# Strassen's scheme for the second layer's second product, in two of its three pairs of token blocks

## The chip, the cores and the metric

The kernel runs on one core of one Trainium2 chip. The metric is the device time of one execution in microseconds, as the median of several executions.

## The reference

Three stages follow each other. An attention with keys and values pooled by 8 (4 x 8 heads, 576 positions, 64 wide) gives x with 2304 rows and 512 columns. A gated layer follows. The last stage is a mixture of 8 experts whose weights per token come from eight rounds of normalisation:

```python
x = _moe_ref(x)                      # (sigmoid(x @ w_gate) * (x @ w_val)) @ w_out, 512 -> 1536 -> 512
N, D = x.shape                       # 2304, 512
P = exp(logits - max); 8 rounds of row and column normalisation      # logits = x @ w_gate, (N, 8)
out = np.zeros((N, D))
for e in range(E):                   # E = 8
    h = np.maximum(x @ w1[e], 0.0)   # 512 -> 1024: the first product
    ye = h @ w2[e]                   # 1024 -> 512: the second product
    out += P[:, e:e + 1] * ye
```

All is float32. The kernel reaches that accuracy on TensorE by splitting each operand into a high and a low half (type float32r) and by adding three products of halves: high x high, high x low and low x high (`PASSES`, L252).

## The kernel before, in words

**Tiling.** The 2304 tokens are six blocks of 384 (`TB`), taken in three pairs. The last stage ("second layer") runs in 96 steps, `steps2` (L657): for each pair of blocks p, each expert e and each quarter q of the expert's hidden columns one step n. The hidden quarter is 2 x 128 columns. Pair 0 is steps 0 to 31, pair 1 steps 32 to 63, pair 2 steps 64 to 95.

**First product.** In a step, x @ w1 for two blocks of tokens, two halves of the inner width and two halves of the hidden quarter is a 2 x 2 by 2 x 2 product of blocks. It is made by the Strassen-Winograd scheme with seven products instead of eight: P1, P5, P6, P3, P7, P2, P4, in this order, called by `product` (L887). Each is 2 (inner) x 3 (passes) = 6 matmuls with 128 x 128 weights and 384 moving columns. The sums of x for it, `xf` (seven tiles a pair, loaded at the end of the pair before by `load_xf`, L714, as soon as the product that reads the old tile is done), come from a scratch memory in DRAM. The sums of w1 are made in each step for the next step by `prep_w1` (L675): ScalarE makes the high halves, GpSimd the sums and the low halves, into the tiles `fa` and `fs`. The raw w1 is loaded two steps ahead by `load_w1` (L661).

**Evacuation.** The results of the products meet in PSUM: `c1`, `c5` and `c2` are copied to SBUF by ScalarE (L1003, L1011, L1018) and added back by VectorE (L1024, L1030, L1037). `hidden` (L905) makes the two halves of the Relu of each block, the high one on ScalarE (L909), the low one on VectorE (L910).

**Second product.** `y_chunk` (L914) makes for one tile of 128 tokens the whole h @ w2 of one hidden quarter: 2 (hidden halves) x 3 (passes) = 6 matmuls, the h tile as weights and 512 columns of w2 moving, into one PSUM bank ("big", four of them). VectorE then adds it, times P, to the accumulator `acc` (L955, first time L941). A step has six such chunks, those of the step before, one behind each of six of the seven products. w2 is split by `prep_w2` (L703): ScalarE makes the high half (L708), VectorE the low one (L709). It is loaded one step ahead by `load_w2` (L667). After the last step the last six chunks run by themselves.

**Order.** The order of the instructions on every engine is the order of this program text (a manual schedule). All DMAs are issued by SP, in order; an issue that waits for a buffer or for a result holds back those behind it. In the first twelve steps the normalisation of P (`sinkhorn`, L833) runs between the chunks.

Of the kernel before, what the change touches and what calls it, by code (L numbers as in the profile page):

```python
# [20 lines left out]
def attention_moe_moe_kernel(  # L21
# [31 lines left out]
    nc = tc.nc  # L53
# [22 lines left out]
    SCALE = 1.0 / (D**0.5) / POOL  # L76

    const = ctx.enter_context(tc.tile_pool(name="const", bufs=1))
    xring = ctx.enter_context(tc.tile_pool(name="xring", bufs=1))
# [5 lines left out]
    def bank(tag, bufs):  # L85
        return ps.tile([128, 512], F32, tag=tag, name=tag, bufs=bufs)
# [11 lines left out]
    def f32(ap):  # L98
        return ap.bitcast(F32)
# [557 lines left out]

    steps2 = [(p, e, q) for p in range(NPAIR) for e in range(E) for q in range(QF)]
    raw1, raw2, wsum, w2hl = {}, {}, {}, {}

    def load_w1(n):  # L661
        if n < len(steps2):
            _, e, q = steps2[n]
            raw1[n] = pools["late"].tile([128, 4, 2, 128], F32, tag="raw1", name="raw1", bufs=2)
            nc.sync.dma_start(out=raw1[n].rearrange("p a k f -> p (a k f)"), in_=moe2_w1[e, q])

    def load_w2(n):  # L667
        if n < len(steps2):
            _, e, q = steps2[n]
            raw2[n] = pools["more"].tile([128, 2, DM], F32, tag="raw2", name="raw2", bufs=2)  # L670
            nc.sync.dma_start(
                out=raw2[n], in_=moe2_w2[e].rearrange("(h g p) d -> g p h d", h=2, p=128)[q]
            )

    def prep_w1(n):  # L675


        if n >= len(steps2):
            return
        raw = raw1.pop(n)  # L680
        pool = pools["more" if n % 2 else "late"]
# [19 lines left out]
        yield  # L701

    def prep_w2(n):  # L703
        raw = raw2.pop(n)
        t = pools["more"].tile([128, 2, 2, DM], F32R, tag="w2hl", name="w2hl", bufs=2)
        w2hl[n] = t
        for i in range(2):
            nc.scalar.activation(out=t[:, 0, i], in_=raw[:, i], func=AF.Copy)  # L708
            nc.vector.tensor_sub(out=t[:, 1, i], in0=raw[:, i], in1=f32(t[:, 0, i]))  # L709
            yield  # L710

    xf = {}

    def load_xf(p, i):  # L714
        if p < NPAIR:
            xf[p, i] = pools["late"].tile([128, 2, 2, TB], F32R, tag=f"xf{i}", name=f"xf{i}", bufs=1)
            nc.sync.dma_start(out=f32(xf[p, i]).rearrange("p s k c -> p (s k c)"), in_=xd[p][i])

    with tc.manual_schedule():
# [152 lines left out]
        c_of = {}  # L872

        def c_tile():
            return pools["more"].tile([128, TB], F32, tag="c", name="c", bufs=5)

        PRODUCTS = {
            "P1": ((0, 0), 0),
# [35 lines left out]
        def y_chunk(n, t):  # L914
# [50 lines left out]
        for n, (p, e, q) in enumerate(steps2):  # L965
            last_of_pair = (e, q) == (E - 1, QF - 1)
            pa = bank("at", 2)
            pc = bank("gv", 2)
# [2 lines left out]
            if n == 0:  # L971
                product(n, "P5", pc, True)
                x2_step(*prev)
                base_pool.__exit__(None, None, None)
                pools["more"] = ctx.enter_context(
                    tc.tile_pool(name="more", bufs=1, side="right", reuse_waits="tile")
                )
                load_w2(0)
                gate = chain(gate, after_block(NBLK - 1, True))
                sk = sinkhorn()  # L980
            load_w2(n + 1)
            load_w1(n + 2)
            prep = prep_w1(n + 1)
# [126 lines left out]
```

## Time and profile before

| | us |
|---|---|
| median of 3 executions | 2157.08 |
| lowest, highest | 2155.01, 2158.38 |
| the profiled execution, its time | 2157.53 |
| its span, first to last instruction | 2155.7 |
| TensorE busy (share of the span) | 2083.4 (97%) |
| VectorE busy | 1349.1 (63%) |
| ScalarE busy | 802.9 (37%) |
| GpSimd busy | 791.0 (37%) |
| moved by DMA | 270.81 MB, mean 126 GB/s |

In the profile PE is TensorE's matmul, PEld its weight load, DVE is VectorE, ACT ScalarE, POOL GpSimd, SP the engine that issues the DMAs. A busy time is the time during which at least one instruction of the engine ran; matmuls overlap each other in the records, so the distance of their starts says more than their duration. The second layer begins at about 633 us.

### The profile page before, as it was taken

What the parts mean: (1) busy time and instruction counts of PE and PEld (TensorE: products, weight loads), DVE (VectorE), ACT (ScalarE), POOL (GpSimd) and SP (SyncE); (2) the same over time, 40 slices, a digit from 0 to 9 for tenths busy, and PEclk for the clock granted to TensorE, in tenths of its full rate; (3) what the DMA queues carried; (4) which work ended last, traced back from release to release, by engine and by line L of the source; (5) the groups of instructions that cost most, each with busy time, mean ns of one, the idle gap of its engine ahead of it and who ended that gap; (6) DMA issues with size and microseconds to landing.
All of it is one profiled execution on the core that took longest, in us unless ns stands there. A gap on an engine that the chain in (4) does not pass through costs nothing.

```text
span 2155.7 us, 28264 instructions
## 1 busy us (share of the span) xinstructions
PE 2083.4 (97%) x10973; PEld 1895.9 (88%) x10973; DVE 1349.1 (63%) x2090; ACT 802.9 (37%) x1457; POOL 791.0 (37%) x712
## 2 busy tenths in 40 slices
PE   4689999999999999999999999999999999999999
PEld 4578999989998888888888898988988898988988
DVE  6836783423226786666666666666666666666665
ACT  4333332223224444334343433434333433434342
POOL 1100001011224474444545444444545444444541
PEclk8699999999999999999999999999999999999999
DMA  7556767776962232211225121211215121221211
GB/s 231 173 179 193 260 230 247 258 246 226 357 235 76 75 107 74 76 62 62 76 83 186 59 79 59 71 66 60 78 59 210 59 79 59 69 68 59 78 59 40
DMA packets 87446, 270.81 MB, mean 126 GB/s; under 512 B 8848, under 2 KB 8848, under 8 KB 87312
## 3 DMA queue, kind: packets, MB, share of 16 engines
q1 hardware_dynamic: 87312, 269.01, 36.7%
q8 instruction: 86, 1.41, 0.3%
q14 instruction: 48, 0.39, 0.1%
HBM read 228.87 MB, written 40.11 MB: 125 GB/s over the span
## 4 chain that ended last, share of the span: by engine, by line
PE 91%; DVE 3%; issue 2%; DMA 2%; ACT 1%; POOL 0%; SPq 0%; DVEq 0%; ACTq 0%; POOLq 0%
PE big L926 37%; PE at L895 19%; PE gv L895 14%; PE gv L260 12%; PE big L552 6%; PE at L343 1%; PE at L429 1%; DMA wide<-in_moe_w_gate_dram 1%; PE at L414 1%; DMA wide<-in_moe_w_val_dram 0%; PE at L260 0%; DVE wa L228 0%; DVE made L163 0%; DVE wide L172 0%; DMA words<-wa 0%
## 5 line engine op out<-in xcount | busy, mean ns | idle before, releaser
L926 PE MATMUL big<-w2hl,h 128*128 128x512 f32 x3456 | 893.2, 394 | 0.0
L926 PEld LDWEIGHTS big<-w2hl,h 128*128 128x128 f32 x3456 | 641.6, 188 | 101.9
L955 DVE SCALAR_TENSOR_TENSOR acc<-big,prob,acc 128x512 f32<-128x512 f32 x516 | 385.5, 747 | 264.9 <-PE big L926 258.8
L260 PE MATMUL gv<-xs,wa 128*128 128x384 f32 x1728 | 339.0, 350 | 29.8 <-DVE wa L228 8.9
L697 POOL TENSOR_TENSOR fa<-raw,fa 128x768 fp32r<-128x768 f32 x96 | 179.5, 1870 | 464.2 <-PE big L926 403.2
L260 PEld LDWEIGHTS gv<-xs,wa 128*128 128x128 f32 x1728 | 311.9, 196 | 37.7 <-DVE wa L228 11.1
L699 POOL TENSOR_TENSOR fs<-ss,fs 128x512 fp32r<-128x512 f32 x96 | 125.1, 1303 | 303.6 <-ACT fs L696 303.6
L895 PE MATMUL at<-xf,fa 128*128 128x384 f32 x1152 | 232.5, 337 | 0.8 <-DVE c L1030 0.8
L895 PE MATMUL at<-xf,fs 128*128 128x384 f32 x1152 | 232.4, 336 | 0.4 <-ACT c L1003 0.4
L895 PE MATMUL gv<-xf,fs 128*128 128x384 f32 x1152 | 231.6, 336 | 0.0
L709 DVE TENSOR_TENSOR w2hl<-raw,w2hl 128x512 fp32r<-128x512 f32 x192 | 227.6, 1186 | 4.7 <-ACT w2hl L708 4.7
L909 ACT ACTIVATE h<-gv 128x384 fp32r<-128x384 f32 x192 | 94.3, 491 | 355.2 <-DVE gv L1037 196.3
L895 PEld LDWEIGHTS at<-xf,fa 128*128 128x128 f32 x1152 | 205.7, 188 | 17.7 <-DVE c L1030 1.6
L895 PEld LDWEIGHTS gv<-xf,fs 128*128 128x128 f32 x1152 | 205.4, 188 | 16.3
L895 PEld LDWEIGHTS at<-xf,fs 128*128 128x128 f32 x1152 | 204.4, 188 | 9.0 <-ACT c L1003 0.7
L910 DVE SCALAR_TENSOR_TENSOR h<-gv,h 128x384 fp32r<-128x384 f32 x192 | 107.1, 558 | 107.6 <-ACT h L909 107.6
L552 PE MATMUL big<-h,wa 128*128 128x384 f32 x864 | 168.0, 344 | 0.0
L552 PEld LDWEIGHTS big<-h,wa 128*128 128x128 f32 x864 | 155.2, 194 | 1.1 <-issue 0.3
L586 POOL TENSOR_TENSOR fx<-x,fx 128x768 fp32r<-128x768 f32 x10 | 18.4, 1836 | 344.8 <-ACT fx L585 323.7
L813 DVE TENSOR_TENSOR g<-g,gv 128x384 f32<-128x384 f32 x72 | 39.7, 551 | 151.9 <-PE gv L260 151.9
L700 POOL TENSOR_TENSOR fs<-ss,fs 128x512 fp32r<-128x512 f32 x96 | 125.4, 1307 | 0.0
L708 ACT ACTIVATE w2hl<-raw 128x512 fp32r<-128x512 f32 x192 | 120.7, 629 | 0.0
(141 smaller groups left out, 2088.6 us busy)
## 6 DMA issues: line engine op xcount, KB each, us to landing
raw<-in_moe_w_dram SPq DMA_DIRECT2D x192, 512.0 KB
wa<-words SPq DMA_DIRECT2D x150, 512.0 KB
words<-wa SPq DMA_DIRECT2D x36, 512.0 KB
xd<-fx SPq DMA_DIRECT2D x21, 768.0 KB
xf<-xd SPq DMA_DIRECT2D x21, 768.0 KB
wide<-in_moe_w_gate_dram SPq DMA_DIRECT2D x12, 512.0 KB
wide<-in_moe_w_val_dram SPq DMA_DIRECT2D x12, 512.0 KB
wide<-in_moe_w_out_dram SPq DMA_DIRECT2D x12, 512.0 KB
```

Source lines behind the costliest of these rows:

```text
L260: nc.tensor.matmul(out=out_, lhsT=a[s], rhs=b[m], start=(i == 0), stop=(i == n - 1))
L552: nc.tensor.matmul(out=x2p[d][:, :TB], lhsT=w[s][:, d * 128 : (d + 1) * 128], rhs=gs[j, f][m], start=(first and i == 0), stop=(last and i ...
L697: pl(out=fa[:, 1], in0=raw[:, 0:3], in1=f32(fa[:, 0]), op=ALU.subtract)
L699: pl(out=fs[:, 1, 0:2], in0=ss[:, 0:2], in1=f32(fs[:, 0, 0:2]), op=ALU.subtract)
L700: pl(out=fs[:, 1, 2:4], in0=ss[:, 2:4], in1=f32(fs[:, 0, 2:4]), op=ALU.subtract)
L708: nc.scalar.activation(out=t[:, 0, i], in_=raw[:, i], func=AF.Copy)
L709: nc.vector.tensor_sub(out=t[:, 1, i], in0=raw[:, i], in1=f32(t[:, 0, i]))
L895: nc.tensor.matmul(out=pt[:, :TB], lhsT=w[:, s, i, k], rhs=t[:, o, k], start=(start and m == 0), stop=(m == 5), skip_group_check=True,)
L909: nc.scalar.activation(out=t[:, 0], in_=src, func=AF.Relu)
L910: nc.vector.scalar_tensor_tensor(out=t[:, 1], in0=src, scalar=0.0, in1=f32(t[:, 0]), op0=ALU.max, op1=ALU.subtract)
L926: nc.tensor.matmul(out=py, lhsT=h[:, s, cs], rhs=w2hl[n][:, o, fh], start=(m == 0), stop=(m == 5))
L955: nc.vector.scalar_tensor_tensor(out=acc[t], in0=py, scalar=pr, in1=acc[t], op0=ALU.mult, op1=ALU.add)
```

## The change

Steps 0 to 31 (pair 0) keep their form, with three additions: the prepared tiles `fa`, `fs` and the split `w2hl` of each of the 32 (e, q) are stored to scratch in DRAM (`fad`, `fsd`, `w2d`). The output of pair 0 is stored by GpSimd's queue instead of SP's.

From step 32 (`NOLD`) on, a new function `step` takes the place of the loop's body:

- w1 is no longer loaded raw and prepared; `fa` and `fs` of the next step are loaded ready from the scratch (0.79 and 1.05 MB a step).
- The second product runs over two steps (two hidden quarters of the same expert) together, with the Strassen-Winograd scheme: the 2 x 2 blocks are the two token blocks by the two hidden halves, times the two hidden halves by the two 256-column halves of w2. Seven products x three tiles of 128 tokens are 21 units (`y_unit`), each of 2 (quarters) x 3 (passes) = 6 matmuls with 256 moving columns. The units of one couple of steps run in the next couple, `PER_SLOT` of them behind each of the 14 first products (none to two).
- The sums of hidden blocks that the scheme wants (s1, n2, s3, s4) are made after the first products by `h_sum`: VectorE makes the sum, ScalarE its high half, GpSimd its low half. a11, a12 and a22 are split as `hidden` did.
- The partial results stand in the two column halves of one PSUM bank for each token tile; `add_to` adds them to the accumulator five times a couple and tile (three times 256 columns, twice 512).
- The blocks of w2: b11, b21 and b22 are loaded split from `w2d`. The sums t1, nt2, t3 and nt4 are made in pair 1 from raw w2 (`rawp`), in place by GpSimd, split by ScalarE and GpSimd and stored to `tsd`; in pair 2 they are loaded from there. `PREP` says in which slot each of these is done.
- At step 32 the six chunks of step 31 run in one block, and the pools "more" and "xring" are closed and replaced by one, "third". Steps 32 and 33 have no units beside their products. After step 95 the last 21 units run by themselves.

```diff
@@ prep_w1, prep_w2, load_w1, load_w2
-        if n < len(steps2):
+        if n < NOLD:
...
+        if n >= NOLD:
+            fa = pool.tile([128, 2, 3, 2, 128], F32R, tag="fa", name="fa", bufs=1)
+            fs = pool.tile([128, 2, 4, 2, 128], F32R, tag="fs", name="fs", bufs=1)
+            wsum[n] = fa, fs
+            nc.sync.dma_start(out=f32(fa).rearrange("p s a k f -> p (s a k f)"), in_=fad[n % NOLD])
+            nc.sync.dma_start(out=f32(fs).rearrange("p s a k f -> p (s a k f)"), in_=fsd[n % NOLD])
+            return
...
+        nc.sync.dma_start(out=fad[n], in_=f32(fa).rearrange("p s a k f -> p (s a k f)"))
+        nc.sync.dma_start(out=fsd[n], in_=f32(fs).rearrange("p s a k f -> p (s a k f)"))
...
+        nc.sync.dma_start(out=w2d[n], in_=f32(t).rearrange("p s h d -> p (s h d)"))
@@ prep_piece: loads, sums and stores of the blocks of w2
+    PREP = {
+        1: (("nt4", "load", 1),),
+        3: (("", "raw", 0), ("nt4", "store", 1)),
+        4: (("b11", "load", 0),),
+        6: (("t1", "sum", 0), ("t3", "sum", 0)),
+        7: (("nt2", "sum", 0),),
+        8: (("t1", "load", 0), ("nt4", "sum", 0)),
+        9: (("nt2", "load", 0),),
+        10: (("t3", "load", 0), ("t1", "store", 0)),
+        11: (("b22", "load", 0), ("nt2", "store", 0)),
+        12: (("t3", "store", 0),),
+        13: (("b21", "load", 0),),
+    }
@@ y_chunk
-                nc.sync.dma_start(out=out[tt * 128 : (tt + 1) * 128], in_=acc[t])
+                nc.gpsimd.dma_start(out=out[tt * 128 : (tt + 1) * 128], in_=acc[t])
@@ new functions
+        def h_sum(n, name, bufs, src, other, op):
+            x = pools["more"].tile([128, TB], F32, tag="hs", name="hs", bufs=4)
+            nc.vector.scalar_tensor_tensor(out=x, in0=src, scalar=0.0, in1=other, op0=ALU.max, op1=op)
+            t = h_tile(n, name, bufs)
+            def low():
+                nc.gpsimd.tensor_tensor(out=t[:, 1], in0=x, in1=f32(t[:, 0]), op=ALU.subtract)
+            def high():
+                nc.scalar.activation(out=t[:, 0], in_=x, func=AF.Copy)
+                owed.append(low)
...
+        UNITS = [(h, w, col, i) for h, w, col in (
+                ("a11", "b11", 0), ("s1", "t1", 1), ("n2", "nt2", 0), ("s3", "t3", 0),
+                ("a22", "nt4", 0), ("s4", "b22", 1), ("a12", "b21", 0)) for i in range(TPB)]
+        PER_SLOT = (2, 1, 2, 2, 2, 1, 1, 2, 2, 2, 1, 1, 2, 0)
...
+        def y_unit(n0, u):
+            h, w, col, i = UNITS[u]
+            if u < TPB:
+                banks[i] = bank("big", 4)
+            pt = banks[i]
+            o = pt[:, col * DH : (col + 1) * DH]
+            first = h in ("a11", "a12")
+            m = 0
+            for k in range(2):
+                for s, b in PASSES:
+                    nc.tensor.matmul(
+                        out=o,
+                        lhsT=hp[n0 + k, h][:, s, i * 128 : (i + 1) * 128],
+                        rhs=pieces2[n0, w][:, k, b],
+                        start=(first and m == 0), stop=(m == 5), skip_group_check=True)
+                    m += 1
+            if h == "a11":
+                add_to(n0, 0, i, o, (0,))
+            elif h == "n2":
+                add_to(n0, 0, i, o, (1,))
+            elif h == "s3":
+                add_to(n0, 1, i, o, (1,))
+            elif h == "a22":
+                add_to(n0, 1, i, pt, (0, 1), True)
+            elif h == "a12":
+                add_to(n0, 0, i, pt, (0, 1), True)
+        def step(n):
...
+            product(n, "P7", pa, False)
+            nc.vector.tensor_tensor(out=vc, in0=va, in1=c5, op=ALU.add)
+            low = h_direct(n, "a22", 3, vc)
+            s1, high = h_sum(n, "s1", 2, vc, a21, ALU.add)
+            high()
+            low()
+            settle(0)
+            done(4, 6)
+            if n != NOLD:
+                product(n, "P2", pb, True)
+            nc.vector.tensor_tensor(out=vb, in0=vb, in1=c1, op=ALU.add)
+            low = h_direct(n, "a11", 2, vb)
+            n2, high = h_sum(n, "n2", 2, vb, s1, ALU.subtract)
+            high()
+            s3, high = h_sum(n, "s3", 3, vb, a21, ALU.subtract)
+            high()
+            low()
+            settle(0)
+            done(5, 1)
+            product(n, "P4", pa, False)
+            low = h_direct(n, "a12", 3, va)
+            s4, high = h_sum(n, "s4", 3, va, n2, ALU.add)
+            high()
+            low()
+            settle(0)
+            done(6, 5)
@@ the loop
+            if n >= NOLD:
+                if n == NOLD:
+                    for t in (3, 4, 5, 0, 1, 2):
+                        y_chunk(n - 1, t)
+                    third()
+                step(n)
+                continue
@@ the end
-        for t in (3, 4, 5, 0, 1, 2):
-            y_chunk(len(steps2) - 1, t)
+        prep_piece(len(steps2) - 2, "nt4", "load")
+        for u in range(len(UNITS)):
+            y_unit(len(steps2) - 2, u)
```

## Rows read from the trace of the kernel before

**Rows 1.** The page's part 1: busy us (share of the span) and instructions.

```profile
PE 2083.4 (97%) x10973; PEld 1895.9 (88%) x10973; DVE 1349.1 (63%) x2090; ACT 802.9 (37%) x1457; POOL 791.0 (37%) x712
```

**Rows 2.** Busy time by stretch: the stage ahead, and steps from 700 us on.

```profile
core 0: us, PE busy (x) PEld busy (x) DVE busy (x) ACT busy (x) POOL busy (x), PEclk, DMA share, GB/s
0.00:630.00 630.00, 568.06 (x3419) 535.87 (x3420) 321.76 (x569) 194.41 (x374) 61.54 (x47) 0.95 0.71 239
...
700.00:2141.70 1441.70, 1441.70 (x7185) 1296.15 (x7184) 976.18 (x1422) 576.98 (x1027) 698.69 (x637) 1.00 0.23 78
```

**Rows 3.** The chain that ended last, its end: start us, us, what.

```profile
2138.37 1.06 PE gv L895 x6
2139.43 1.39 PE big L926 x6
2140.82 1.04 PE at L895 x6
2141.86 9.58 PE big L926 x42
2151.44 0.02 issue
2151.47 0.75 DVE acc L955
```

**Rows 4.** TensorE in order of time: the same product in two following steps.

```profile
1135.97 1.22 PE L895 MATMUL gv<-xf,fa 128*128 128x384 f32 x6
...
1151.62 1.21 PE L895 MATMUL gv<-xf,fa 128*128 128x384 f32 x6
```

**Rows 5.** Busy time by stretch, columns as in rows 2: two steps.

```profile
1300.00:1331.30 31.30, 31.30 (x158) 28.14 (x157) 20.88 (x30) 12.37 (x23) 15.17 (x14) 1.00 0.21 68
```

**Rows 6.** Groups by line in these two steps: xcount | busy us, mean ns.

```profile
L955 DVE SCALAR_TENSOR_TENSOR acc<-big,prob,acc 128x512 f32<-128x512 f32 x12 | 9.0, 747 | 6.3 <-PE big L926 6.2
L709 DVE TENSOR_TENSOR w2hl<-raw,w2hl 128x512 fp32r<-128x512 f32 x4 | 4.8, 1190 | 0.0
L910 DVE SCALAR_TENSOR_TENSOR h<-gv,h 128x384 fp32r<-128x384 f32 x4 | 2.2, 558 | 2.2 <-ACT h L909 2.2
L910 DVE SCALAR_TENSOR_TENSOR h<-c,h 128x384 fp32r<-128x384 f32 x2 | 1.6, 807 | 1.2 <-ACT h L909 1.2
L1024 DVE TENSOR_TENSOR gv<-gv,c 128x384 f32<-128x384 f32 x2 | 1.1, 567 | 0.7 <-PE gv L895 0.7
L1037 DVE TENSOR_TENSOR gv<-gv,c 128x384 f32<-128x384 f32 x2 | 1.1, 550 | 0.0
...
L708 ACT ACTIVATE w2hl<-raw 128x512 fp32r<-128x512 f32 x5 | 3.1, 627 | 0.0
L909 ACT ACTIVATE h<-gv 128x384 fp32r<-128x384 f32 x4 | 2.0, 492 | 7.2 <-DVE gv L1037 4.0 <-DVE gv L1024 3.2
L909 ACT ACTIVATE h<-c 128x384 fp32r<-128x384 f32 x2 | 1.1, 526 | 2.2 <-DVE c L1030 2.2
L1003 ACT COPY c<-at 128x384 f32<-128x384 f32 x2 | 1.0, 480 | 4.0 <-PE at L895 4.0
...
L700 POOL TENSOR_TENSOR fs<-ss,fs 128x512 fp32r<-128x512 f32 x2 | 2.6, 1298 | 0.0
L691 POOL TENSOR_TENSOR ss<-raw 128x256 f32<-128x256 f32 x2 | 1.5, 740 | 0.0
```

**Rows 7.** Busy time by stretch, columns as in rows 2: three with many transfers.

```profile
500.00:560.00 60.00, 60.00 (x383) 57.08 (x382) 19.50 (x33) 16.56 (x31) 7.38 (x4) 1.00 0.77 251
...
1130.00:1145.00 15.00, 15.00 (x76) 13.54 (x76) 9.79 (x16) 5.66 (x11) 7.29 (x7) 1.00 0.96 352
...
570.00:590.00 20.00, 20.00 (x117) 18.97 (x116) 3.83 (x7) 4.53 (x8) 6.50 (x6) 1.00 1.02 415
```

**Rows 8.** SP's queue in order of time at the border of pairs 0 and 1.

```profile
1126.42 13.55 SPq L717 DMA_DIRECT2D xf<-xd  x7
...
1144.26 13.54 SPq L959 DMA_DIRECT2D out_dram<-acc  x6
```

**Rows 9.** Weight loads: a group of the page, and a burst in order of time.

```profile
L895 PEld LDWEIGHTS gv<-xf,fs 128*128 128x128 f32 x1152 | 205.4, 188 | 16.3
...
384.54 0.96 PEld L343 LDWEIGHTS at<-kp,qt 64*128 64x128 f32 x8
```

More of the change, by code (lines that the diff above doesn't have):

```diff
@@ L710, in prep_w2, with load_pair @@
             yield
+        nc.sync.dma_start(out=w2d[n], in_=f32(t).rearrange("p s h d -> p (s h d)"))
+        yield
+    DH = DM // 2
+    pieces2 = {}
+    rawp = {}
+    def load_pair(n0):
+        if n0 < 2 * NOLD:
+            rawp[n0] = pools["more"].tile([128, 2, 2, DM], F32, tag="rawp", name="rawp", bufs=1)
+            for i in range(2):
+                _, e, q = steps2[n0 + i]
+                nc.sync.dma_start(
+                    out=rawp[n0][:, i], in_=moe2_w2[e].rearrange("(h g p) d -> g p h d", h=2, p=128)[q]
+                )
@@ L874, in c_tile @@
         def c_tile():
-            return pools["more"].tile([128, TB], F32, tag="c", name="c", bufs=5)
+            return pools["more"].tile([128, TB], F32, tag="c", name="c", bufs=c_bufs[0])
+        c_bufs = [5]
         PRODUCTS = {
@@ L958, in y_chunk, with settle, h_tile @@
             if (e, q) == (E - 1, QF - 1):
-                nc.sync.dma_start(out=out[tt * 128 : (tt + 1) * 128], in_=acc[t])
+                nc.gpsimd.dma_start(out=out[tt * 128 : (tt + 1) * 128], in_=acc[t])
+        hp = {}
+        owed = []
+        def settle(k):
+            while owed and len(owed) > k:
+                owed.pop(0)()
+        def h_tile(n, name, bufs):
+            hp[n, name] = pools["more"].tile([128, 2, TB], F32R, tag=name, name=name, bufs=bufs)
+            return hp[n, name]
@@ new lines, in attention_moe_moe_kernel, with add_to @@
+        UNITS = [
+            (h, w, col, i)
+            for h, w, col in (
+                ("a11", "b11", 0),
+                ("s1", "t1", 1),
+                ("n2", "nt2", 0),
+                ("s3", "t3", 0),
+                ("a22", "nt4", 0),
+                ("s4", "b22", 1),
+                ("a12", "b21", 0),
+            )
+            for i in range(TPB)
+        ]
+        PER_SLOT = (2, 1, 2, 2, 2, 1, 1, 2, 2, 2, 1, 1, 2, 0)
+        banks = {}
+        def add_to(n0, half, i, src, cols, done=False):
+            p, e, q = steps2[n0]
+            t = half * TPB + i
+            tt = p * CPP + t
+            pr = prob[:, tt, e : e + 1]
+            if (p, t) not in acc2:
+                acc2[p, t] = pools["more"].tile([128, DM], F32, tag="acc", name="acc", bufs=6), set()
+            a, seen = acc2[p, t]
+            todo = [d for d in cols if d not in seen]
+            if todo and len(todo) < len(cols):
+                for d in cols:
+                    add_to(n0, half, i, src[:, (d - cols[0]) * DH : (d - cols[0] + 1) * DH], (d,))
+            else:
+                o = a[:, cols[0] * DH : (cols[-1] + 1) * DH]
+                if todo:
+                    nc.vector.tensor_scalar_mul(out=o, in0=src, scalar1=pr)
+                    seen.update(cols)
+                else:
+                    nc.vector.scalar_tensor_tensor(out=o, in0=src, scalar=pr, in1=o, op0=ALU.mult, op1=ALU.add)
+            if done and (e, q) == (E - 1, QF - 2):
+                nc.sync.dma_start(out=out[tt * 128 : (tt + 1) * 128], in_=a)
+                del acc2[p, t]
@@ new lines, in y_slot, with done @@
+        def y_slot(n, k):
+            k += 7 * (n % 2)
+            n0 = n - n % 2 - 2
+            if n0 >= NOLD:
+                u = sum(PER_SLOT[:k])
+                for i in range(PER_SLOT[k]):
+                    y_unit(n0, u + i)
+            for name, part, lag in PREP.get(k, ()):
+                prep_piece(n - n % 2 - 2 * lag, name, part)
+        def step(n):
+            p, e, q = steps2[n]
+            last_of_pair = (e, q) == (E - 1, QF - 1)
+            pa = bank("at", 2)
+            pc = bank("gv", 2)
+            pb = bank("gv", 2)
+            load_w1(n + 2)
+            prep = prep_w1(n + 1)
+            def done(k, x=None):
+                if x is not None and last_of_pair:
+                    load_xf(p + 1, x)
+                if n >= NOLD:
+                    y_slot(n, k)
+                next(prep, None)
+            va, vb, vc = (t[:, :TB] for t in (pa, pb, pc))
+            product(n, "P1", pa, True)
+            c1 = c_tile()
+            nc.scalar.copy(out=c1, in_=va)
+            done(0, 0)
+            product(n, "P5", pc, True)
+            c5 = c_tile()
+            nc.scalar.copy(out=c5, in_=vc)
+            done(1, 3)
+            if n == NOLD:
+                product(n, "P2", pb, True)
+            product(n, "P6", pa, False)
+            c2 = c_tile()
+            nc.scalar.copy(out=c2, in_=va)
+            done(2, 4)
+            product(n, "P3", pc, False)
+            nc.vector.tensor_tensor(out=vc, in0=vc, in1=c2, op=ALU.add)
+            a21 = pools["more"].tile([128, TB], F32, tag="a21", name="a21", bufs=2)
+            nc.scalar.activation(out=a21, in_=vc, func=AF.Relu)
+            done(3, 2)
+            product(n, "P7", pa, False)
[7 more added lines that the diff above has]
+            if n != NOLD:
+                product(n, "P2", pb, True)
+            nc.vector.tensor_tensor(out=vb, in0=vb, in1=c1, op=ALU.add)
[14 more added lines that the diff above has]
+            done(6, 5)
```

91 lines of the change are left out of this document (85 added, 6 removed).

## The prediction

> **What bounds the kernel now.** I read first the page's busy times, then the busy times by stretch, then the chain that ended last, and last the groups by line. TensorE is busy for 97% of the span and no other engine for more than 63% [rows 1]. The stretches place it: from 700 to 2141.7 us, the second layer, TensorE is busy for all of 1441.7 us at a granted clock of 1.00, the higher of its two levels, while VectorE, the next one, is busy for 976 us [rows 2]. A full "busy" of TensorE need not mean that it never waits, so I check the chain: in the last steps it holds nothing but matmuls, in groups of six, a first product in 1.04 or 1.06 us and a chunk of the second product in 1.39 us, up to the last add [rows 3]. One step is seven products and six chunks; the same product returns after 1151.62 - 1135.97 = 15.65 us [rows 4]. So here only fewer or cheaper matmuls shorten the time, as long as the other engines stay ahead.
>
> **Prices of a matmul.** A chunk costs 1.39/6 = 231.7 ns for each matmul of 512 columns. The products cost (15.65 - 6 x 1.39)/7 = 1.044 us, 174.0 ns for each of 384 columns. After the last product 36 chunk matmuls run with little beside them: (9.58 - 1.39)/36 = 227.5 ns [rows 3, 4]. No row shows 256 columns, the new width. The line through 174.0 and the quiet 227.5 has 0.418 ns a column and gives 120.5 ns at 256; the line through 174.0 and 231.7 gives 116.3 ns. The 512-column matmuls lose 4.2 ns to their neighbours in a step; if the short ones lose as much, they cost 124.7 ns. I take 120.5, because its line has a fixed part (about 13 ns each) that twice as many matmuls must pay, and keep 116.3 and 124.7 as ends.
>
> The page "TensorE: Matmul & The Clock Gate" of the Trainium skill, section "Back-to-back issue gap", gives 262 cycles for 256 columns, about 109 ns at 2.4 GHz. The same rule would put 384 columns at 162.5 ns, where the rows have 174.0, so the trace disagrees; by the rule the sum below would gain 93 us and end near 2070 us.
>
> **Second product, pairs 1 and 2 (steps 32 to 95).** Removed: 64 steps x 36 = 2304 matmuls of 512 columns: 2268 x 231.7 + 36 x 227.5 ns = 533.7 us. Added: per two steps 7 products x 3 token tiles x 6 = 126 matmuls of 256 columns, for 32 such couples 4032: x 120.5 ns = 485.9 us. Gain 47.8 us, all on the path; at 116.3 ns it is 64.8 us, at 124.7 ns 30.9 us. A couple of steps goes from 31.30 to 2 x 7.31 + 126 x 0.1205 = 29.8 us. The first products are the same 42 matmuls a step, costed at no change.
>
> **VectorE.** Per step three adds into PSUM (567, 567, 550 ns), three low halves and four sums of the hidden blocks at 558 ns: 5.59 us. Per couple of steps `add_to` has nine 256-wide adds (the line through 558 at 384 and 747 at 512 gives 369 ns) and six 512-wide ones at 747 ns: 7.80 us. Together 2 x 5.59 + 7.80 = 19.0 us in 29.8 us, against 20.9 in 31.3 now, since the w2 splits (4 x 1190 ns) go [rows 5, 6]. A sum could cost the 807 ns of the form with both operands in SBUF; then it is 21.0 us. Still covered; without cover each 369 ns add would cost its own length.
>
> **ScalarE and GpSimd.** ScalarE: per step three copies of 480 ns, four Relu of 492 and four high halves at 526: 5.5 us, so 11.0 us a couple, plus 4 x 627 ns in pair 1; now 12.4 [rows 5, 6]. GpSimd: eight 384-wide low halves (between 740 at 256 and 1298 at 512: 1019 ns), and in pair 1 four sums and four low halves of w2 at 1298: 18.5 us of 29.8, against 15.2 now; in pair 2 only 8.2. The w1 preparation is gone from step 32 on. All of this is hidden under TensorE: the results are used a step or more later.
>
> **Transfers.** In pair 0 every step also stores 0.79 + 1.05 MB of prepared w1 and 1.05 MB of split w2: with the two loads 3.9 MB in 15.65 us, 251 GB/s. In pair 1 a couple loads 3.67 MB of w1, 1.57 MB of w2 quarters and 1.05 MB of raw w2 and stores 2.1 MB: 8.4 MB in 29.8 us, 281 GB/s; in pair 2 246 GB/s. The queues have carried 352 GB/s at a share of 0.96 (367 at full share) and 415 at 1.02, and at 251 GB/s TensorE was busy for all of 60 us [rows 7]. So they fit, at some 70 to 80%. On SP's queue each store waits for its producer and holds the loads behind it; these are wanted a step later, so I cost the stores at 0, with 3 us as upper end. A gain is excluded, as no transfer limits this stretch. The output stores of pair 0 move from SP, where six of them stretched over 13.54 us [rows 8], to GpSimd's queue: nothing waits for SP there, and six issues on GpSimd delay its low halves by little: 0.
>
> **The border of pairs 0 and 1.** The chunks of step 31 now run in one block before step 32, and steps 32 and 33 have first products only. A step then has 7.3 us of matmuls and 5.6 us each on VectorE and ScalarE, in one chain. After P3 come an add (567), a Relu (492) and another add (567), 1.6 us, before P4 may write; P7 covers 1.04, so some 0.6 us plus the handovers is lost in step 32 (P2 covers it in 33). ScalarE then has eight hidden halves to do (4.1 us after P7) before it copies the next c1, which P6 waits for, behind 3.1 us of other matmuls and P4: 1 to 2 us. The w1 of step 33 (1.8 MB, about 5 us at 367 GB/s) has 7 us. I take 5 us, with 1 and 12 as ends, the upper for late w1 and w2 loads and for memory handed over from the old pools. At the border of pairs 1 and 2 the seven xf tiles (5.5 MB, issued over 13.55 us [rows 8]) meet about 4.2 MB of the new traffic: 9.7 MB at 367 to 415 GB/s is 23 to 26 us, and the last tile is wanted about 27 us after the first issue. I take 1 us, ends 0 and 5.
>
> **The end.** The last 21 units follow the last step; their matmuls are in the 4032. The last add (0.75 us) and store stay.
>
> **The sum**, against the profiled execution (2157.5 us, span 2155.7, within 0.5 us of the median 2157.1): 2157.5 - 47.8 + 5 + 1 = 2115.7, say 2116 us. With the ends: 2157.5 - 64.8 + 1 = 2094 and 2157.5 - 30.9 + 20 = 2147.
>
> **Rivals.** (a) The weight loads set the pace. Each matmul brings its own load of 128 columns, recorded at 188 ns [rows 9], and 256 columns stream in less. If one start must follow the other by that record, 4032 x 188 = 758 us: +224, so about 2388 us, slower. It decides from (533.7 - 6)/4032 = 130.9 ns a matmul on. For it: no row has a stream that short with 128 rows and columns. Against: loads already start every 174 ns, and in the scores' burst, where the moving part is 72 columns, eight loads start within 0.96 - 0.19 us, one each 110 ns [rows 9]. 110 is below 120.5, but by only 10 ns. Chance 0.08. Beside it stands a rule of the same page of the skill, section "What overlaps and what doesn't": a load overlaps with running matmuls only in another row group. By it a 384-column matmul would take 174 + 110 ns, which the rows deny.
> (b) TensorE waits in every step: `add_to` sits in VectorE's queue between the hidden blocks, and the last three slots of an odd step bring it about 7.3 us of work (5.0 of hidden blocks, 3 x 0.747) in 5.3 us of matmuls (3 x 1.044 + 3 x 0.72). It has the next slots to catch up, and the low half of a11 is wanted some 4 us after P2, by my count with 1 us to spare. If 0.45 us a step is lost, 64 x 0.45 = 29 us: 2145 us; at 0.65 us the gain is gone. Chance 0.17.
> (c) The short matmul costs 116.3 ns or less: 2099 us. Chance 0.17.
> (d) Transfers bind in pair 1: the quarters come in short rows (256 elements). At 250 GB/s, 8.4 MB take 33.6 us, 3.8 more than the couple has; 16 couples lose 60: 2176 us. Chance 0.05.
>
> **How the numbers follow.** The forecast (2104 to 2130) has 0.50, (c) 0.17, (b) 0.17, (a) 0.08, (d) 0.05, and 0.03 is for a disturbance in the stage ahead. A measurement here can tell about 0.2% (4 us) from no change. Faster: 0.50 + 0.17 + 0.13 of (b) + 0.03 = 0.83. Same: 0.03. Slower: (a), (d) and the rest of (b), 0.14. The range 2092 to 2148 holds the forecast, most of (c) and (b), about 0.8.
>
> **What would show it.** Steps 34 to 95: couples of 29.8 us; groups of six 256-column matmuls in 0.72 us (0.70 and 0.75 at the ends, over 0.785 for no gain); no wait of TensorE in the waits view there; VectorE about 64% busy. Between steps 31 and 34: idle TensorE of about 5 us. Transfer share 0.7 to 0.8 in pair 1. Wrong if the groups take over 0.75 us, or if a TensorE wait comes back in each couple.

## The result and the profile after

The changed kernel takes 2122.26 us (median of 4, 2120.67 to 2123.10), the kernel before beside it 2156.49 us: a ratio of 0.984, 95% interval 0.9823 to 0.9857. The forecast was 2116 us, range 2092 to 2148. The profiled execution took 2122.35 us with a span of 2120.5; before it was 2157.53 and 2155.7.

Page of the changed kernel, part 1, beside [rows 1]:

```profile
PE 2036.5 (96%) x12701; PEld 1945.8 (92%) x12701; DVE 1255.1 (59%) x2256; ACT 773.9 (36%) x1521; POOL 728.8 (34%) x654
```

There are 1728 more matmuls, and TensorE is busy for 47 us less. The other engines lose work too. Busy time by stretch, columns as in [rows 2]: around the border of pairs 0 and 1, and the steps behind it:

```profile
1133.00:1170.00 37.00, 32.03 (x161) 28.29 (x160) 17.69 (x31) 11.26 (x24) 14.17 (x16) 1.00 0.92 365
1170.00:2100.00 930.00, 926.85 (x6516) 923.81 (x6514) 556.46 (x1093) 355.73 (x746) 405.95 (x372) 1.00 0.77 270
```

TensorE is full again behind the border, now with transfers at a share of 0.77. A couple of steps, in order of time on TensorE (P1 of an even step, the units behind it, P1 two steps later):

```profile
1335.71 1.21 PE L996 MATMUL at<-xf,fa 128*128 128x384 f32 x6
1336.76 0.88 PE L1148 MATMUL big<-t,s 128*128 128x256 f32 x6
1337.48 0.88 PE L1148 MATMUL big<-nt,a 128*128 128x256 f32 x6
...
1365.55 0.69 PE L996 MATMUL at<-xf,fa 128*128 128x384 f32 x3
```

The couple takes 1365.55 - 1335.71 = 29.84 us against 2 x 15.65 = 31.30 [rows 4], a unit 1337.48 - 1336.76 = 0.72 us. From start to start the new matmul takes 119.8 ns in the mean of all 4032.

Laid out by the starts of P1, from the two profiled executions (us):

| stretch | before | changed | without waits |
|---|---|---|---|
| steps 0 and 1 | 34.6 | 35.8 | |
| steps 2 to 30 | 457.1 | 457.0 | |
| step 31, with the chunks behind it | 15.7 | 23.9 | |
| steps 32 to 35 | 62.6 | 52.1 | 44.3 |
| steps 36 to 63 | 438.5 | 418.0 | 415.7 |
| steps 64 and 65 | 31.3 | 32.2 | 29.7 |
| steps 66 to 94 | 454.1 | 433.5 | 430.9 |
| step 95 to the start of the last matmul | 23.6 | 31.6 | 29.6 |
| from there to the end | 4.7 | 4.1 | |

Step 0 starts at 633.5 us before and at 632.2 after; in the profiled executions of this study it starts anywhere from 628 to 641 us, so small differences are read from the stretches and not from whole times. "Without waits" is 14.62 us for the products of two steps and 29.70 for a couple, which a later experiment reached. The matmuls save 533.7 - 4032 x 0.1198 = 50.7 us; the column's differences, 7.8 + 2.3 + 2.5 + 2.6 + 2.0 = 17.2 us, are given back as waits. 50.7 - 17.2 = 33.5 us, within 2 us of the measured 35.2. So the question is where the 17 us come from; the forecast had 6 us of waits.

TensorE's waits in the changed kernel from 1100 us on (us in total, times, longest):

```profile
PE at L996 <- ACT c L1199: 2.5, 1, 2.5
PE big L1148 <- DVE a L1077: 1.9, 2, 1.1
PE at L996 <- DMA fa<-fad: 1.9, 1, 1.9
PE at L996 <- DVE gv L1217: 1.8, 2, 0.9
PE big L1148 <- DVE acc L1130: 0.8, 1, 0.8
PE at L996 <- ACT c L1209: 0.6, 1, 0.6
```

All of them lie at the two borders and at the end. The waits view shows nothing of the steady couples, and yet they are 0.14 us or more longer than they need be (2.3 us over the 14 couples of steps 36 to 63); this shows only when one reads how long before its use each supplier is done.

### The profile page after: what moved, and what is told of

Its sections match the earlier page's. It is cut to its first block, busy times and chain, and to the rows that moved or that the text cites. A ratio compares the mean times of both kernels' runs of the same rounds, so it can differ in the third digit from the quotient of the medians.

```text
span 2120.5 us, 33188 instructions
## 1 busy us (share of the span) xinstructions
PE 2036.5 (96%) x12701; PEld 1945.8 (92%) x12701; DVE 1255.1 (59%) x2256; ACT 773.9 (36%) x1521; POOL 728.8 (34%) x654
## 4 chain that ended last, share of the span: by engine, by line
PE 88%; DVE 5%; DMA 3%; issue 2%; ACT 2%; POOL 0%; SPq 0%; DVEq 0%; ACTq 0%; POOLq 0%
PE big L1148 22%; PE at L996 18%; PE gv L996 14%; PE big L1027 12%; PE gv L261 12%; PE big L553 6%; PE at L344 1%; PE at L430 1%; DMA words<-wa 1%; DVE wa L229 1%; DMA fa<-fad 1%; PE at L415 1%; DMA wide<-in_moe_w_val_dram 0%; PE at L261 0%; DMA b<-w2d 0%
## 5 line engine op out<-in xcount | busy, mean ns | idle before, releaser
L1087 POOL TENSOR_TENSOR s<-hs,s 128x384 fp32r<-128x384 f32 x192 | 195.1, 1017 | 411.1 <-ACT s L1090 260.9
L1027 PE MATMUL big<-w2hl,h 128*128 128x512 f32 x1152 | 296.9, 394 | 0.0
L1130 DVE SCALAR_TENSOR_TENSOR acc<-big,prob,acc 128x256 f32<-128x256 f32 (+1 forms) x462 | 254.7, 586 | 45.1 <-PE big L1148 45.1
L1027 PEld LDWEIGHTS big<-w2hl,h 128*128 128x128 f32 x1152 | 213.8, 188 | 34.4
L996 PEld LDWEIGHTS at<-xf,fa 128*128 128x128 f32 x1152 | 198.5, 188 | 11.2 <-DVE gv L1217 2.4
L1148 PE MATMUL big<-t,s 128*128 128x256 f32 x1152 | 162.7, 282 | 0.8 <-DVE acc L1130 0.8
L1148 PE MATMUL big<-b,a 128*128 128x256 f32 x1152 | 159.0, 283 | 2.1 <-DVE a L1077 1.9
L1148 PEld LDWEIGHTS big<-t,s 128*128 128x128 f32 x1152 | 157.1, 189 | 1.0 <-DVE acc L1130 1.0
L1148 PEld LDWEIGHTS big<-b,a 128*128 128x128 f32 x1152 | 153.6, 190 | 3.0 <-DVE a L1077 2.9
L1056 DVE SCALAR_TENSOR_TENSOR acc<-big,prob,acc 128x512 f32<-128x512 f32 x144 | 107.6, 748 | 70.8 <-PE big L1027 68.8
L1090 ACT ACTIVATE s<-hs 128x384 fp32r<-128x384 f32 x192 | 100.5, 523 | 110.6 <-DVE hs L1083 110.6
```

What stands on the lines that cost most here:

```text
L996: nc.tensor.matmul(out=pt[:, :TB], lhsT=w[:, s, i, k], rhs=t[:, o, k], start=(start and m == 0), stop=(m == 5), skip_group_check=True,)
L1027: nc.tensor.matmul(out=py, lhsT=h[:, s, cs], rhs=w2hl[n][:, o, fh], start=(m == 0), stop=(m == 5))
L1056: nc.vector.scalar_tensor_tensor(out=acc[t], in0=py, scalar=pr, in1=acc[t], op0=ALU.mult, op1=ALU.add)
L1087: nc.gpsimd.tensor_tensor(out=t[:, 1], in0=x, in1=f32(t[:, 0]), op=ALU.subtract)
L1090: nc.scalar.activation(out=t[:, 0], in_=x, func=AF.Copy)
L1130: nc.vector.scalar_tensor_tensor(out=o, in0=src, scalar=pr, in1=o, op0=ALU.mult, op1=ALU.add)
```

## The experiments

**What a narrow matmul costs.** The forecast's price rested on a line, and its slower rival on the weight load.

```diff
@@ y_unit, last couple only
+            wide = 256 if n0 < len(steps2) - 2 or u < 6 else 192 if u < 12 else 128 if u < 18 else 64
-                        out=o, ... rhs=pieces2[n0, w][:, k, b],
+                        out=o[:, :wide], ... rhs=pieces2[n0, w][:, k, b, :wide],
```

> Only the last 21 units, which run alone after the last step, are changed: units 0 to 5 keep 256 moving columns, units 6 to 11 have 192, 12 to 17 have 128, 18 to 20 have 64, so the last couple leaves out part of its sums. The changed kernel has 120.0 ns a matmul at 256 columns there, and two theories give that number: (1) the line, columns / 2.4 GHz + 13.3 ns (173.3 at 384, 227 at 512): then 192, 128 and 64 columns take 93.3, 66.7 and 40.0 ns; (2) the weight load: a load of 128 columns starts at best every 110 ns, or 107 + 13.3 = 120 ns. Then 192, 128 and 64 columns all take 110, or all 120 ns. By (1) the time falls by 36 x 26.7 + 36 x 53.3 + 18 x 80 ns = 4.3 us against the changed kernel, by (2) at 110 ns by 0.9 us, at 120 ns by nothing. I expect 93.3 to be cut off at about 110 ns: the line as long as it is above the load, the load below it.

TensorE in order of time, this kernel's last units (18 matmuls a row):

```profile
2101.68 2.42 PE L1149 MATMUL big<-t,s 128*128 128x256 f32 x18 [0.82 <-DVE acc L1130]
2103.94 2.16 PE L1149 MATMUL big<-nt,n 128*128 128x192 f32 x18
2105.93 2.17 PE L1149 MATMUL big<-t,s 128*128 128x192 f32 x18
2107.94 2.14 PE L1149 MATMUL big<-nt,a 128*128 128x128 f32 x18
2109.92 2.18 PE L1149 MATMUL big<-b,s 128*128 128x128 f32 x18
2111.94 2.14 PE L1149 MATMUL big<-b,a 128*128 128x64 f32 x18
```

Its one execution took 2119.80 us; a single time decides nothing between 0.9 and 4.3 us, the rows do. From row to row 18 matmuls of 192 columns take 1.99 and 2.01 us, of 128 columns 1.98 and 2.02: 111 ns each, and the starts of the 64-column ones are 112 ns apart. At 256 columns they are 120 ns apart. Both theories hold, each on its side: the line (13.3 ns beside the columns) down to where it meets a floor, then 111 ns, whatever the width. That the floor is the weight load fits a burst in the changed kernel, where loads of 64 x 64, each with 72 moving columns, start closer together:

```profile
66.04 1.02 PE L344 MATMUL at<-kp,qt 64*64 64x72 f32 x16
66.99 0.79 PE L553 MATMUL big<-h,wa 128*128 128x384 f32 x3
```

These 16 pairs of a load and a matmul start within 66.99 - 66.04 = 0.95 us, 59 ns each, so handing out a pair is not what takes 111 ns; that it is the load itself, and not something else of the pair, is argued. 256 columns stand 9 ns above the floor; rival (a) missed by that. A further halving of the columns, with 7/4 as many matmuls again at 111 ns each instead of 120, would be slower (an estimate from these rows).

**One part of the change alone.** The kernel before, with w1 prepared once and loaded ready in pairs 1 and 2.

```diff
@@ load_w1, prep_w1 (as in the change); second product as before
+        if n >= NOLD:
+            ... nc.sync.dma_start(out=fa, in_=fad[n % NOLD]); nc.sync.dma_start(out=fs, in_=fsd[n % NOLD])
+            return
```

> The kernel before with one part of the change alone: w1 is prepared in pair 0 only, stored, and loaded ready in pairs 1 and 2; the second product stays as it was. Theory (what lies under TensorE's matmuls costs nothing and gives nothing): 2157 us, within 3 us, with steps of 15.65 us, GpSimd nearly idle from step 32 on, and a loss of 0 to 2 us at the two borders. Rival 1: the work taken off GpSimd and ScalarE makes the 512-column matmuls cheaper (they take 231.7 ns in a step and 227.5 with little beside them): up to 36 x 4.2 ns x 64 steps = 9.7 us, 2147 us. Rival 2: the added traffic (to some 250 GB/s in pair 0, 180 in the others) slows the matmuls or makes them wait: over 2162 us.

2157.09 us against 2158.87 for the kernel before, ratio 0.9991 (0.9982 to 1.0001); steps of 15.64 and 15.67 us, no wait at a border. Busy time by stretch, columns as in [rows 2]:

```profile
1170.00:1640.00 470.00, 470.00 (x2343) 422.36 (x2342) 277.88 (x451) 135.10 (x270) 0.00 (x0) 1.00 0.43 155
```

GpSimd has nothing left to do (0.00), ScalarE a quarter less, and the time is the same: what lies under the matmuls is worth nothing by itself. It also excludes that the 512-column matmuls lost their 4 ns to GpSimd; of ScalarE's work only a quarter was taken away, and that gave nothing. So the gain is the matmuls'.

**How close the other engines run.** The forecast counted 1 us to spare in the crowded end of a step (rival b).

```diff
@@ h_sum
+            for _ in range(2):
                 nc.vector.scalar_tensor_tensor(out=x, in0=src, scalar=0.0, in1=other, op0=ALU.max, op1=op)
```

> Each of the four sums of hidden blocks on VectorE is made twice (same operands, same result): four more instructions of 0.56 us in a step, all in its crowded last three slots, VectorE's work in a couple of steps from 17.8 to 22.3 us of 29.84. Theory (only the total counts, the queue catches up in the next slots): steady couples stay at 29.84 us, 2122 us, with at most 2 us more at the border and the end. Rival (the prediction's count of 1 us to spare before the low half of a11 is wanted): the low half comes 1.7 us later, so some 0.7 us is lost at the first unit of each couple, 31 couples: about 22 us, 2144 us, and TensorE's waits name the low half of a11.

2259.29 us: steady couples of 34.08 us, 4.24 us longer, for 4 x 2 x 0.56 = 4.5 us of added work. Both expectations missed, the rival by a factor of six. VectorE is busy for 65% of this kernel's steady stretch. Its largest waits of TensorE:

```profile
PE big L1149 <- DVE a L1077: 50.2, 32, 2.3
PE big L1149 <- DVE acc L1131: 40.0, 57, 1.2
PE at L996 <- ACT c L1200: 17.1, 31, 3.9
```

Almost all of the added work shows in the time: there is no slack. The reason is in the unaltered changed kernel. First its busy time, columns as in [rows 2], from the hidden blocks of an odd step to the adds behind them:

```profile
1347.46:1355.20 7.74, 7.74 (x55) 7.68 (x54) 7.07 (x14) 4.04 (x9) 5.01 (x5) 1.00 0.93 317
```

VectorE, busy for 60% of the couple, is busy for 91% of this stretch. Then the end of the odd step, all engines in order of time:

```profile
1351.18 0.55 DVE L1077 SCALAR_TENSOR_TENSOR a<-gv,a 128x384 fp32r<-128x384 f32 x1
1351.29 1.59 PE L1148 MATMUL big<-b,a 128*128 128x256 f32 x12
...
1352.96 0.55 DVE L1083 SCALAR_TENSOR_TENSOR hs<-at,hs 128x384 f32<-128x384 f32 x1
...
1353.55 0.53 ACT L1090 ACTIVATE s<-hs 128x384 fp32r<-128x384 f32 x1 [1.34 <-DVE hs L1083]
...
1353.98 0.46 ACT L1199 COPY c<-at 128x384 f32<-128x384 f32 x1
...
1354.49 1.33 PE L996 MATMUL at<-xf,fs 128*128 128x384 f32 x6
```

The low half of a11 (first row) ends at 1351.73; unit 0, begun at 1351.29, wants it in its sixth matmul, at 1351.89: 0.16 us to spare. c1 of the new step (L1199) stands in ScalarE's queue behind the high half of s4, which waits for s4 on VectorE, which stands behind two of the accumulator's adds. It ends at 1354.44, P6 starts at 1354.49, and its group lasts 1.33 us instead of 1.21. P6, P3 and P7 of this step feed the next round of the same hidden blocks. The theory: a loop through three queues, as long as TensorE's own couple. The next runs tested it.

```diff
@@ step
+            h_direct(n, "a11", 2, vb)()                  # low half at once, ahead of n2 and s3
-            low = h_direct(n, "a11", 2, vb)  ...  low()
@@ s4: its high half waits until c1 of the next step is copied
-            high()
+            held.append(high)
...
             nc.scalar.copy(out=c1, in_=va)
+            release()                                    # the held high halves, then their low halves
```

> The changed kernel, with two changes of order only: the low half of a11 is made on VectorE right after its high half, ahead of the sums n2 and s3; and the high half of s4 waits on ScalarE until c1 of the next step is copied. Theory (a closed loop): the copy c1 of a step waits on ScalarE for the high half of s4 of the step before, that for VectorE's queue, that for P7 of the step before, and P6, P3, P7 wait for c1; the trace has c1 ready 0.05 us before P6 wants it in every even step, and the low half of a11 0.16 us before its use, so TensorE runs at the loop's own pace. Expected: the long first matmul of P6 goes, couples from 29.84 to 29.73 us (31 x 0.11 = 3.4 us), step 33, which has nothing but the loop, from 12.47 to about 11.5, together 2117 to 2119 us. Rival (the total of VectorE's work counts, 60% busy, no loop): 2122 us, couples unchanged.

2114.63 us (2110.77 to 2117.33), ratio 0.9804 (0.9788 to 0.9821). Couples are 29.70 us in place of 29.84: steps 36 to 63 take 415.7 us instead of 418.0, steps 66 to 94 430.9 instead of 433.5. ScalarE in order of time, the same place:

```profile
1352.25 0.47 ACT L1205 COPY c<-at 128x384 f32<-128x384 f32 x1
1353.23 0.53 ACT L1096 ACTIVATE s<-hs 128x384 fp32r<-128x384 f32 x1 [0.51 <-DVE hs L1089]
```

c1 is ready at 1352.72, and P6 starts at 1354.24. It is shown that the order of the queues cost each steady couple its 0.14 us. Both changes were made in one run; that c1 and not a11 was the late one rests on the rows above, where a11 had 0.16 us to spare. Step 33 did not follow: 12.78 us, where 11.5 was expected.

The same order with the sums twice:

> The same two changes of order, with each of the four sums made twice as in the run that lost 4.24 us a couple. Loop theory: the second sums of n2, s3 and s4 no longer stand ahead of the low half of a11 and of c1; what is left is the reading of PSUM by the accumulator's adds behind them (40 us of 107 in that run's waits). The loss falls to under 2.2 us a couple, at most 2190 us. Rival (VectorE's throughput in the crowded slots is what lacks, whatever the order): the loss stays at 4 us a couple, 2250 us or more.

2235.01 us; couples of 33.27 us, 3.57 above 29.70. Neither theory has this number, and the rival (4 us) is the nearer. The waits for a11 and c1 are gone from the steady couples, as the loop theory says, and one that it undervalued takes nearly all of their place. The wait, and the busy time of a stretch with two such waits (columns as in [rows 2]):

```profile
PE big L1155 <- DVE acc L1137: 77.1, 119, 1.7
...
1407.30:1416.00 8.70, 7.94 (x53) 7.30 (x52) 8.04 (x16) 4.33 (x10) 4.01 (x4) 1.00 0.91 329
```

A unit may write into its PSUM columns only when the add before has read them, and that add stands in VectorE's queue behind the hidden blocks. VectorE is busy for 67% of the steady stretch, but for 8.04 of the 8.70 us in this row: in the crowded slots it is nearly full, which is what the rival says. Whether another order could loosen it was not tried.

**The border of pairs 0 and 1.** First theory: c1 of step 33 behind step 32's hidden blocks.

```diff
@@ step, n == NOLD only
+                nc.vector.tensor_tensor(out=vb, in0=vb, in1=c1, op=ALU.add); h_direct(n, "a11", 2, vb)()   # ahead of P3
...
+                product(n + 1, "P1", pa2, True); nc.scalar.copy(out=early[n + 1][1], in_=pa2[:, :TB])      # ahead of a12
```

> The changed kernel loses 1.1, 5.2 and 1.4 us in steps 32, 33 and 34 against steps without waits. Theory: VectorE and ScalarE hand the hidden blocks of step 32 back and forth in one chain, and c1 of step 33 waits behind it in ScalarE's queue (2.53 us of idle TensorE at P6). Here, in step 32 alone, the add of c1 and the split of a11 move ahead of P3, and P1 of step 33 with its copy c1 moves ahead of the split of a12. Expected: the 2.53 us wait at P6 of step 33 falls to under 0.5, steps 32 to 34 together get 2.5 to 4 us shorter, 2118 to 2120 us. Rival: the border waits for its transfers (w1 of step 33, raw w2), for which a chain made shorter changes nothing: the same 2122 us, with TensorE waiting for a DMA at P1 or P5 of step 33.

2121.94 us; steps 32 to 34 took 37.16 us instead of 37.60. The 2.5 us wait for c1 went, as expected, and others came in its place (c2 1.7 us, c5 0.8 us): the theory named a wait, not the cause. In this run's step 33 the granted clock also fell, to 0.57 from 1165 to 1169 us, after TensorE had idled for 1.67 us; P4 followed 1.06 us after the start of the add that frees its columns, against 0.62 us in the changed kernel, so the clock hid some 0.4 us of the gain, not the 2 us that lacked. In the changed kernel the next rows behind that wait, all engines in order of time, show more:

```profile
1162.36 1.31 PE L996 MATMUL at<-xf,fs 128*128 128x384 f32 x6 [2.53 <-ACT c L1199]
1162.98 4.01 POOL L794 TENSOR_TENSOR rawp<-rawp 128x512 f32<-128x512 f32 x3
...
1164.30 0.63 ACT L774 ACTIVATE t<-rawp 128x512 fp32r<-128x512 f32 x1 [1.62 <-POOL rawp L794]
1164.84 0.46 ACT L1209 COPY c<-at 128x384 f32<-128x384 f32 x1
...
1165.35 1.33 PE L996 MATMUL at<-xf,fs 128*128 128x384 f32 x6 [0.65 <-ACT c L1209]
...
1167.02 0.63 ACT L774 ACTIVATE nt<-rawp 128x512 fp32r<-128x512 f32 x1 [1.72 <-POOL rawp L794]
```

The splits of t1 and nt2 stand on ScalarE ahead of c2 (L1209) and a21 and wait for GpSimd's sums. The last run moved them:

```diff
@@ PREP (on the kernel with order and late stores, below)
-        8: (("t1", "load", 0), ("nt4", "sum", 0)),
-        9: (("nt2", "load", 0),),
-        10: (("t3", "load", 0),),
-        11: (("b22", "load", 0),),
+        8: (("nt4", "sum", 0),),
+        9: (("t1", "load", 0),),
+        11: (("nt2", "load", 0), ("b22", "load", 0)),
+        12: (("t3", "load", 0),),
```

> The kernel of the run before (order and late stores), with the splits of t1, nt2 and t3 on ScalarE and GpSimd moved from slots 8, 9 and 10 of a couple to 9, 11 and 12. Theory on what is left of the border: in step 33 ScalarE's queue stands at the split of t1, then of nt2, which wait for GpSimd's sums of raw w2 (1.62 and 1.72 us in the changed kernel), and c2 and a21 of the step stand behind them, so TensorE waits at P7 and P4. Expected: c2 no longer behind a split, step 33 from 12.8 us to 11 to 11.8, steady couples at 29.70 us, 2110 to 2112 us. Rival 1: step 33 is bound by its chain of VectorE and ScalarE alone: 12.8 us as before. Rival 2: the splits now stand in ScalarE's crowded slots and hold up c1 of the next step: the couples of pair 1 (not of pair 2) get longer than 29.70 us.

Step 33 takes 9.79 us instead of 12.80, more than was expected, and steps 32 to 35 48.7 instead of 51.4 (52.1 in the changed kernel); the couples keep 29.70 us. The granted clock fell to 0.57 for 4 us in step 33 of the kernel compared with, but in the one with the order alone it stayed at 1.00 there, and the step took 12.78 us all the same. ScalarE in order of time in step 33 of this kernel:

```profile
1173.45 0.48 ACT L1217 COPY c<-at 128x384 f32<-128x384 f32 x1 [0.25 <-PE at L997]
1174.22 0.63 ACT L774 ACTIVATE t<-rawp 128x512 fp32r<-128x512 f32 x1 [0.29 <-POOL rawp L794]
```

c2 now waits 0.25 us for TensorE alone. So 3.0 us of step 33, and 2.7 of the border's 7.8, were w2's splits in ScalarE's queue; neither rival holds.

**The border of pairs 1 and 2.** The seven xf tiles meet the new traffic; TensorE waited 1.9 us for the w1 of step 65. Is it the engines or SP's order?

```diff
@@ run 1: PREP
-        10: ... ("t1", "store", 0)   11: ... ("nt2", "store", 0)   12: (("t3", "store", 0),)
+        2: (("t1", "store", 1),)     5: (("nt2", "store", 1),)     7: ... ("t3", "store", 1)
@@ run 2: prep_w1
-            nc.sync.dma_start(out=fa, in_=fad[n % NOLD])       # and fs
+            nc.scalar.dma_start(out=fa, in_=fad[n % NOLD])
```

> At the border of pairs 1 and 2, step 64 takes 17.53 us where other even steps take 15.30, and TensorE waits 1.87 us for the w1 of step 65. Theory A: the 16 DMA engines are full there (share 1.02 at 398 GB/s from 1619 to 1637 us). Here the stores of t1, nt2 and t3 (0.52 MB each) come a couple of steps later, which takes 1.5 MB out of steps 62 and 63. Expected by A: step 64 gets at least 1.5 us shorter, 2120 us; the steady couples stay at 29.84 us. Theory B: SP's queue is what is late (the load of w1 is issued 6 us after the start of step 64, behind a store and a load that wait). By B the share may fall, but the load is issued no earlier than 3 us after the start, and at least 1 us of the wait stays.

> The loads of the prepared w1 (fa, fs) are issued by ScalarE's queue instead of SP's, so they no longer stand behind stores and loads that wait. Theory B (SP's queue is late at step 64): the load of step 65 is issued within 2 us of the start of step 64, the wait of 1.87 us goes, 2120 us. Theory A (the DMA engines are full): issued earlier, it still shares the full engines with the tiles of xf; the wait falls by less than half, 2121 to 2122 us. [...]

Run 1: 2118.10 us; step 64 takes 15.35 us instead of 17.53, but step 65 15.80 instead of 14.63; together 31.15 instead of 32.16, at a share of 1.02. Run 2: 2122.65 us; the load of w1 for step 65 is issued 3.3 us after the start of step 64 instead of 6.3, and step 64 becomes longer, 22.15 us, in the profiled execution. TensorE in step 64 of run 2, in order of time, and a stretch, columns as in [rows 2]:

```profile
1630.73 1.31 PE L996 MATMUL gv<-xf,fa 128*128 128x384 f32 x6 [3.68 <-DMA xf<-xd]
...
1633.93 2.26 PE L996 MATMUL at<-xf,fa 128*128 128x384 f32 x6 [0.89 <-DVE hs L1083]
...
1633.00:1639.00 6.00, 5.11 (x19) 5.10 (x19) 3.29 (x7) 2.12 (x5) 2.98 (x3) 0.50 0.55 199
```

With the engines full, an earlier w1 makes a tile of xf late: theory A. Steps 64 and 65 lose 5.4 us against the changed kernel. Half of it is more idle time (4.6 instead of 1.9 us); the other half is the clock, which behind the wait was granted at 0.50 (1.2 GHz), so that the same matmuls took 33.0 us instead of 30.3.

Run 1 agrees in sign, but less than half of the excess over 29.84 us went. The rest is not settled. Full engines alone do not cost time: the kernel with the splits moved has a share of 1.02 in steps 64 and 65, and they take 29.70 us, nothing lost. Nor is SP's place excluded: that kernel issues the load 4.2 us after the start of step 64, run 1 4.8 us and the changed kernel 6.3 us. What is shown is that later stores take 1.0 us of the loss away, and that an earlier issue by itself adds to it.

**Order and late stores together.**

> The two changes of order together with the stores of t1, nt2 and t3 put off to the next couple, each of which takes away another wait. If they add up: 2122.3 - 3 to 5 (order) - 1.5 to 4 (stores) = 2113 to 2118 us, faster than the kernel before and than the changed one. If the waits replace each other: 2118 us, as with the stores alone.

2112.04 us (2109.28 to 2117.86), ratio to the kernel before 0.9802 (0.9785 to 0.9819): steps 64 and 65 take 30.25 us, the couples 29.70. The waits add up: from step 2 to the last matmul the late stores gain 1.6 us (1446.7 against 1448.3 in the changed kernel), the order 6.0, both 7.6. With the splits moved as well, the second layer from step 0 to the last matmul is 9.0 us shorter than in the changed kernel (1475.14 against 1484.18 us) although steps 0 and 1 happened to take 1.8 us more there. Its ratio to the kernel before is 0.9785 (0.9767 to 0.9804), its median 2115.31 us beside 2159.24. By its ratio this is the best of the kernels run: its interval lies below that of the changed kernel, by about half a per cent in the middle. Against the kernel without the moved splits (0.9785 to 0.9819) the whole times show no sure difference; there the stretches alone speak for it.

## Why the prediction was right, and where not

**What bounds.** Right: TensorE is the bound before and after, and the gain is that of fewer matmul columns. The kernel with w1 prepared once shows the other half: work taken off the other engines, with the matmuls left as they were, gives 0.

**The price of 256 columns.** Taken 120.5 ns, measured 119.8; the line through 384 columns and the quiet 512 was the right one, and the neighbours' 4.2 ns do not come with the narrow matmuls (119.8 in the steps, 120 at the end). The gain of this term is 50.7 us against 47.8. The Trainium skill's page "TensorE: Matmul & The Clock Gate" (section "Back-to-back issue gap") has 262 cycles, 109 ns, for this width, as the gap of an isolated matmul; this stream, with a load for each matmul, has 120, and the measurement decides. Its rule that a load overlaps with running matmuls only in another row group ("What overlaps and what doesn't") is contradicted: one after the other, 107 ns of columns (256 at 2.4 GHz) and a load at the 111 ns of the floor would take 218 ns, and the run has 120. (The prediction's 174 + 110 ns for 384 columns adds the load to a pace that holds it already; 160 + 111 ns would be the sum, and the rows deny that too.)

**The slower rival (a).** Right in its mechanism as far as the rows show, wrong in its size: there is a floor, at 111 ns and not at the 188 ns of the load's record. The burst of [rows 9], 110 ns, was the row to go by.

**Transfers.** Forecast 0.7 to 0.8 of the engines in pair 1 and 281 GB/s; measured 0.81 and 284 from 1200 to 1600 us; no steady couple waits for one.

**Rival (b).** The couples came out at the 29.8 us foreseen, so the rival did not bind. But the step that gave it "1 us to spare" failed: it was 0.16 us for a11, and c1, which the count had not looked at, came too late: the order of the queues already cost 0.14 to 0.18 us a couple, 2.3 + 2.6 = 4.9 us in all. That the couple agrees to 0.04 us is luck: the cheaper matmul (126 x 0.7 ns = 0.09 us) hid most of this wait. The 256-wide add is recorded at 480 ns, not 369: the line through 384 and 512 columns of two different operations did not hold. VectorE's total is smaller all the same, 239.4 of 400 us (60%, 17.9 us a couple, against 19.0), since its records overlap: three such adds in a row take 1.27 us. The forecast lived on a margin that it did not know.

**The borders and the end.** Border of pairs 0 and 1: 5 taken (1 to 12), 7.8 measured; the chain of VectorE and ScalarE was named, the splits of w2 ahead of c2 were not, and they were some 3 us. Border of pairs 1 and 2: 1 taken (0 to 5), 2.5 measured, in a stretch with full engines, as the forecast's 23 to 26 us of transfer in 27 should have warned. The end: nothing taken, 2.0 lost, most of it in two waits of 0.8 us where units follow P4 with no product between them; no run tested this one. With the 4.9 us of the couples it is 17.2 us instead of 6, 11.2 more; the matmuls gave 2.9 us beyond the forecast, which leaves 8.3. The profiled execution missed by 2122.35 - 2115.7 = 6.7 us; the difference lies within the 2 us that the stretches do not account for. So the matmuls' share of the forecast was right by its mechanism, while the waits were taken at a third of what they are; that the number came as near as 6.7 us is in part luck, as the matmuls gave more than was taken.

**What stays open.** Some 4 us of the first border (48.7 against 44.3 us in the best kernel), what at the second border takes the last 1.3 us away, the 2.0 us of the end, and what would free VectorE for the accumulator's adds in the crowded slots; none was tried further.

## What to carry to other kernels

Splitting a product further pays on TensorE only while the price of a matmul falls faster than their number grows: here 7/4 x 119.8 = 210 ns stand against 231.7, and below 111 ns the price fell no further. Take it from two widths in the trace and look for a burst that shows the load alone. When TensorE is full and the others are at 60%, look at each of them in its most crowded stretch and not over the whole step; take the instruction that hands back each buffer and read how long before its use it is done; a loop through three strict queues can be as long as TensorE's own round while no wait is visible. At a border between phases, look first for work of the next phase that stands in a queue ahead of this phase's short copies.

## What was not expected of the hardware

Matmuls of 192, 128 and 64 moving columns with a full 128 x 128 load each start 111 to 112 ns apart, all the same. From 256 columns on the distance is columns / 2.4 GHz + 13.3 ns (120 at 256, 173.3 at 384). With the 16 DMA engines full (share 1.02, 384 GB/s), whole steps ran without a wait; in another kernel, with the loads of w1 issued 3 us earlier by another queue, TensorE waited 3.7 us for another tile, was then granted 0.50 of its clock for 6 us, and two steps took 5.4 us more.
